# Seven products of quarters in both layers, tile 0's second layer in two parts around them, and some weights kept

## The chip, the cores and the metric

The kernel runs on one core of a Trainium2 chip. The metric is the device time of one execution in microseconds (us). TensorE (PE) multiplies into PSUM; LDWEIGHTS (PEld) loads its stationary operand beside it. VectorE (DVE), ScalarE (ACT) and GpSimd (POOL) do elementwise work, and SyncE (SP) issues nearly all DMA transfers from one queue. All engines run their own instruction list in order and wait for each other through semaphores.

## What is computed

Inputs are fp32: q, k, v of 2 batches x 8 heads x 768 positions x 64, and for two layers a w_in of 512x2048 and a w_out of 2048x512. The outline of the reference:

```
scores_l = scale * q @ k.T, kept where |i-j| < 16        # window
scores_s = scale * q @ max_of_32(k).T + log(32)          # block summaries
x = softmax([scores_l, scores_s]) @ [v, mean_of_32(v)]   # x: 1536 x 512
h = x @ moe_w_in;  x = max(h, 0)**2 @ moe_w_out          # layer 0
h = x @ moe2_w_in; out = (h * sigmoid(1.702 * h)) @ moe2_w_out   # layer 1
```

## The kernel before

The 1536 tokens are three tiles of 512 (t = 0, 1, 2), the 2048 hidden columns 16 blocks of 128 (f). Every fp32 operand is split into a high and a low fp32r part (xh and xl, gh and gl, two weight tiles w each), and every product of blocks is three matmuls, hi*hi, hi*lo and lo*hi, of 128x128 on 128x512. One `step(m, t, f)` (L733) is layer m, tile t, block f: 12 matmuls of x with w_in (L743) into one PSUM bank, the activation, the split into gh and gl (L767 to L773), and in `finish()` (L778, one step later) 12 matmuls with w_out (L791 in layer 0, L793 in layer 1), which add to four banks over all 16 blocks.

A weight block is loaded as raw 512 KB (`fetch`, L662), scaled in place by ACT (L678), shifted and merged by DVE (L682, L685), and split by `parts` (L704: a cast on ACT or DVE, L709 or L710, and a subtraction on DVE or POOL, L714). There are 28 weight tiles (`NW`, L630), 16 of them beside the attention and 12 in memory that comes free when it ends; raw blocks have three buffers.

For layer 1, tiles 0 and 1, `pairs` (L866) takes two tiles and two blocks at a time as a 2x2 product of quarters and makes it with seven products instead of eight (L895), each 6 matmuls. Sums of quarters come first (`operands` L819 for the tokens, `prep_pair` L833 for the weights, helper `add` L692). Partial sums pass through bank `a` four times; after each of the first three, `keep` (L911, a copy, mostly on ACT, L307) takes the bank's value before the next product adds to it, and `sum_to` (L903) adds on DVE. The pair's first tile is finished in the loop, the second one in `late` (L946), which holds 12 matmuls per block.

The main sequence (L973 to L990): the attention together with layer 0 of tile 0, in the order of the table `ORDER` (L27; `k`, `q`, `v` are loads, `sv` the block means of v by matmul, L436, `tk` and `tq` transposes, L457, `h` and `t` the two ends of a 128-row attention block, `w` weight blocks, `s` and `S` steps). Then layer 0 of tile 1 and tile 2 in plain steps, `pairs` for layer 1 of tiles 0 and 1, `late` for tile 1, and plain steps for layer 1 of tile 2. A planner (`Plan`, L113) gives each operation a start on its engine from costs written into the kernel, lets `soonest` choose between two engines (`LEAN` adds to DVE's end), and the instructions are emitted in the order of these starts. TensorE also gets small matmuls on a constant (L996) in planned gaps before the first dense work.

Of the kernel before, what the change touches and what calls it, by code (L numbers as in the profile page):

```python
# [10 lines left out]
F32 = mybir.dt.float32  # L11
F32R = mybir.dt.float32r
U32 = mybir.dt.uint32
AF = mybir.ActivationFunctionType
# [13 lines left out]
    k,0,1 k,1,1 sel k,2,1 tk,0 tk,1 q,1,1 q,0,1 tk,2 pk,0 m,1 sv,0 m,0 tq,1 m,2 pk,1 tq,0 v,0 q,3,1 v,1  # L28
    h,0,0 q,2,0 w,3,0 h,0,1 h,3,0 h,1,0 h,1,1 ps,0 t,0 w,0,0 v,2 h,2,0 w,0,1 w,2,0 v,3 h,2,1 h,3,1 t,1 w,2,1
    tq,2 pk,2 s,0,0 w,3,1 v,4 t,2 w,1,0 t,3 s,3,0 h,4,0 k,3,1 s,2,0 s,2,1 w,1,1 tk,3 h,5,0 s,0,1 sv,1 s,3,1  # L30
    s,1,0 w,6,0 v,5 k,5,1 tq,3 k,4,0 w,6,1 w,4,0 tk,4 h,4,1 tk,5 s,1,1 pk,5 S,6 t,4 v,6 w,4,1 h,5,1 w,5,0
    w,5,1 w,10,0 q,4,0 S,4 S,5 w,7,0 v,7 w,10,1 w,7,1 pk,3 S,10 pk,4 t,5 tq,4 S,7 ps,1 w,14,0 w,8,0 h,7,0
    w,8,1 w,9,0 w,11,0 v,8 h,6,0 h,7,1 S,8 h,6,1 h,9,0 w,14,1 S,14 q,5,0 t,7 h,9,1 w,11,1 w,9,1 tq,5 S,11
    t,6 w,12,0 v,9 h,11,0 h,11,1 h,10,0 S,9 t,9 v,10 v,11 w,15,0 w,12,1 h,8,0 S,12 t,11 w,13,0 w,13,1 h,10,1
    h,8,1 w,15,1 S,15 t,10 S,13 t,8
# [77 lines left out]
class Plan:  # L113
# [11 lines left out]
    LEAN = {"DVE": 0.5}  # L125
# [67 lines left out]
    def soonest(self, choices, reads=(), writes=(), after=()):  # L193
# [60 lines left out]
def kernel(  # L254
# [375 lines left out]
    NA, NW = 4 * RING, 4 * RING + 12  # L630
# [6 lines left out]
    def end_attention():  # L637
# [91 lines left out]
    ended = set()  # L729
    first_ops = {}  # L730
    pending = []

    def step(m, t, f, c0, c1, first, last):  # L733
# [14 lines left out]
        wt.release(wih, wil)  # L748
        wt.held |= {woh.name, wol.name}
# [280 lines left out]
```

## Time and profile before

| | |
|---|---|
| median of 3 runs | 599.99 us (599.25 to 603.17) |
| the profiled execution's own time | 599.57 us |
| its span, first to last instruction | 597.8 us |
| mean granted TensorE clock, share of full speed | 0.996 |
| PE busy | 582.0 us, 97% of the span, 3472 matmuls |
| DVE, ACT, POOL busy | 498.8, 418.7, 66.3 us |
| moved by DMA | 104.58 MB, mean 175 GB/s |

The profile is of one execution. Busy times count overlapping instructions of an engine once, and ends of matmuls are modelled, so that waits are read from the list of waits, and the pace of matmuls from the starts in the timeline. "Idle before" names what ended the wait.

### The profile page before, as it was taken

How to read it: one execution, taken by the hardware profiler on the slowest of the kernel's cores; microseconds unless marked ns; L12 is line 12 of the kernel's file. 1: busy time of each engine (PE TensorE's matmuls, PEld its weight loads, DVE VectorE, ACT ScalarE, POOL GpSimd, SP SyncE). 2: the span in 40 equal slices, each digit the busy share in tenths (PEclk: the TensorE clock that was granted, in tenths of full speed). 3: DMA queues.
4: the chain of work that ended last, by engine and by line, in shares of the span. 5: the costliest groups of instructions: out<-in, count | busy, mean ns of one | idle time of the engine just before them, and what ended most of it. 6: DMA issues, size and time to landing. Idle time of an engine off the chain costs nothing.

```text
span 597.8 us, 9872 instructions
## 1 busy us (share of the span) xinstructions
PE 582.0 (97%) x3472; PEld 484.5 (81%) x3472; DVE 498.8 (83%) x1065; ACT 418.7 (70%) x848; POOL 66.3 (11%) x129
## 2 busy tenths in 40 slices
PE   7799999999999999999999999999999999999997
PEld 6588988788888888888888888888888888888885
DVE  4788898879889777698676799999999999899992
ACT  6888797788877777764787776667776545665543
POOL 5121100023110000020001212211110000000000
PEclk9989999999999999999999999999999999999999
DMA  9999988834537655522565513434445766766641
GB/s 242 230 249 261 255 210 234 203 113 132 151 101 242 210 172 186 209 70 70 178 212 194 158 47 108 157 123 133 142 148 182 241 192 214 252 187 200 185 133 70
DMA packets 95313, 104.58 MB, mean 175 GB/s; under 512 B 29792, under 2 KB 82016, under 8 KB 95264
## 3 DMA queue, kind: packets, MB, share of 16 engines
q1 hardware_dynamic: 94944, 103.17, 58.2%
q0 software_dynamic: 320, 0.79, 0.6%
q8 instruction: 27, 0.44, 0.3%
q14 instruction: 22, 0.18, 0.1%
HBM read 100.01 MB, written 3.15 MB: 173 GB/s over the span
## 4 chain that ended last, share of the span: by engine, by line
PE 86%; DMA 7%; ACT 3%; DVE 2%; issue 1%; SPq 0%; POOL 0%; DVEq 0%; ACTq 0%
PE acc L791 12%; PE acc L793 11%; PE acc L743 11%; PE m L793 9%; PE h L743 8%; PE m L743 7%; PE acc L895 7%; PE m L791 5%; PE h L895 4%; DMA raw<-in_moe_w_in_dram 2%; PE m L895 2%; PE h L793 2%; PE h L791 2%; PE m L598 2%; DMA qin<-in_q_dram 1%; DMA kin<-in_v_dram 1%
## 5 line engine op out<-in xcount | busy, mean ns | idle before, releaser
L678 ACT ACTIVATE raw<-raw 128x512 f32<-128x512 f32 x164 | 108.1, 678 | 21.8 <-DMA raw<-in_moe_w_in_dram 11.3
L685 DVE SCALAR_TENSOR_TENSOR xw<-raw,xw 128x512 uint32<-128x512 uint32 x164 | 112.7, 693 | 6.0 <-ACT raw L678 2.0
L714 DVE TENSOR_TENSOR w<-xw,w 128x512 fp32r<-128x512 f32 (+1 forms) x167 | 114.9, 695 | 2.6 <-ACT w L709 0.8
L709 ACT CAST w<-xw 128x512 fp32r<-128x512 f32 (+1 forms) x129 | 77.3, 608 | 36.7 <-DVE xw L685 36.3
L791 PE MATMUL acc<-gh,w 128*128 128x512 f32 (+1 forms) x288 | 81.7, 368 | 1.0 <-DVE xl L611 1.0
L682 DVE TENSOR_SCALAR xw<-raw 128x512 uint32<-128x512 uint32 x164 | 69.6, 426 | 15.1 <-DMA raw<-in_moe_w_out_dram 11.5
L743 PE MATMUL h<-xh,w 128*128 128x512 f32 (+1 forms) x224 | 69.6, 370 | 1.0 <-DVE xl L611 1.0
L771 DVE TENSOR_TENSOR gl<-r,gh 128x512 fp32r<-128x512 f32 (+1 forms) x68 | 45.9, 674 | 25.8 <-ACT gh L769 25.6
L743 PE MATMUL acc<-xh,w 128*128 128x512 f32 x192 | 63.0, 389 | 0.0
L791 PEld LDWEIGHTS acc<-gh,w 128*128 128x128 f32 x288 | 51.9, 188 | 10.1 <-DVE xl L611 1.2
L793 PE MATMUL acc<-w,gh 128*128 128x512 f32 x192 | 59.2, 389 | 0.0
L791 PE MATMUL acc<-gl,w 128*128 128x512 f32 (+1 forms) x144 | 52.7, 366 | 0.0
L793 PE MATMUL m<-w,gh 128*128 128x512 f32 x160 | 49.3, 389 | 0.0
L743 PEld LDWEIGHTS h<-xh,w 128*128 128x128 f32 x224 | 40.7, 188 | 8.5 <-ACT pT L307 1.2
L769 ACT CAST gh<-r 128x512 fp32r<-128x512 f32 (+1 forms) x66 | 39.7, 602 | 6.4 <-DVE r L765 4.8
L793 PEld LDWEIGHTS acc<-w,gh 128*128 128x128 f32 x192 | 36.1, 188 | 7.6
L743 PEld LDWEIGHTS acc<-xh,w 128*128 128x128 f32 x192 | 36.1, 188 | 7.5
L743 PE MATMUL m<-xh,w 128*128 128x512 f32 x128 | 42.0, 389 | 0.0
L743 PE MATMUL h<-xl,w 128*128 128x512 f32 (+1 forms) x112 | 40.3, 360 | 0.0
L793 PE MATMUL acc<-w,gl 128*128 128x512 f32 x96 | 37.3, 389 | 0.0
L743 PE MATMUL acc<-xl,w 128*128 128x512 f32 x96 | 37.3, 389 | 0.0
L558 ACT ACTIVATE sm<-sm,st 128x120 f32<-128x120 f32 x96 | 36.6, 385 | 0.8 <-DVE st L549 0.8
(181 smaller groups left out, 1111.4 us busy)
## 6 DMA issues: line engine op xcount, KB each, us to landing
raw<-in_moe_w_out_dram SPq DMA_DIRECT2D x90, 512.0 KB, 3.7
raw<-in_moe_w_in_dram SPq DMA_DIRECT2D x74, 512.0 KB, 3.9
vw<-in_v_dram SPq DMA_DIRECT2D x20, 192.0 KB, 6.1
kin<-in_v_dram SPq DMA_DIRECT2D x6, 512.0 KB, 7.3
out_dram<-r SPq DMA_DIRECT2D x12, 256.0 KB, 2.1
kin<-in_k_dram SPq DMA_DIRECT2D x5, 512.0 KB, 5.6
qin<-in_q_dram SPq DMA_DIRECT2D x3, 512.0 KB, 7.3
qin<-in_q_dram SPq DMA_DIRECT2D x6, 256.0 KB, 6.7
```

Of the source, the lines that this page charges most:

```text
L558: nc.scalar.activation(out=s.t[:, h, :], in_=s.t[:, h, :], func=AF.Exp, bias=st.t[:, 0, h:h + 1], scale=-1.0, accum_out=st.t[:, 1, h:h + 1])
L678: nc.scalar.activation(out=top, in_=top, func=AF.Prelu, scale=-(2.0 ** -80), alpha=-(2.0 ** -32))
L682: op("DVE", 0.36, lambda: nc.vector.tensor_scalar(out=x.t, in0=raw.t[:, :, 0], scalar1=29, scalar2=None, op0=ALU.logical_shift_right), rea ...
L685: op("DVE", 0.64, lambda: nc.vector.scalar_tensor_tensor(out=x.t, in0=raw.t[:, :, 1], scalar=3, in1=x.t, op0=ALU.logical_shift_left, op1=A ...
L709: plan.soonest([("ACT", 0.09 + 0.44 * fr, False, lambda: nc.scalar.copy(out=hi.t[:, hc], in_=src())), ("DVE", 0.05 + 0.4 * fr, True, lambd ...
L714: eng.tensor_tensor(out=lo.t[:, lc], in0=src(), in1=hi.t[:, hc].bitcast(F32), op=ALU.subtract)
L743: nc.tensor.matmul(hp.t[:, cols], lhsT=w.t[:, kc * P:(kc + 1) * P], rhs=x.t[:, kc, cols], start=(kc == 0 and n == 0), stop=(kc == KC - 1 a ...
L769: ("ACT", da - 0.1, False, lambda: nc.scalar.copy(out=gh.t[:, cols], in_=r.t[:, cols]))],
L771: op("DVE", dd, lambda: nc.vector.tensor_tensor(out=gl.t[:, cols], in0=r.t[:, cols], in1=gh.t[:, cols].bitcast(F32), op=ALU.subtract), rea ...
L791: nc.tensor.matmul(a.t[:, cols], lhsT=w.t[:, j * P:(j + 1) * P], rhs=g.t[:, cols], **st)
L793: nc.tensor.matmul(a.t, lhsT=g.t[:, j * P:(j + 1) * P], rhs=w.t, **st)
L895: nc.tensor.matmul(bank.t, lhsT=a, rhs=rhs(b, kh), start=(begin and k == 0 and n == 0), stop=(k == 1 and n == 2), skip_group_check=True)
```

## The change

Layer 0 of tiles 1 and 2 now goes through `pairs` and `late` too, and layer 1 takes the pair (2, 1). Tile 0's second layer runs in plain steps, in two parts: 10 blocks before layer 0's pairs, 6 behind layer 0's `late`. The first part's output is copied into four tiles `part` and added on DVE at the end (`parted`). While such a part runs, `operands_first` makes the sums of quarters for the pairs that follow and prepares their first weights, one piece per step (`beside`). The first two blocks of each `pairs` use split weights that are still there (`keep_w`, `kept_w`), with sums made from the parts (`add(x0, h0, l0)`); the last pair's w_out stay for `late`, which goes through the blocks backwards; tile 2's fp32 output of layer 0 is copied from PSUM for its sums (`kept`). `pairs` has no step pending when it begins, and prepares the next pair's weights as soon as a pair's own are released. The activation of layer 1 is one ACT instruction (`Gelu_apprx_sigmoid`) instead of a sigmoid on ACT and a multiplication on DVE. The subtraction for gl may go to POOL. Weight tiles are 24 instead of 28. The planner's lean on DVE is split, and becomes 1.5 against ACT and 0.25 against POOL behind the attention. `ORDER` is a new table; what it moves is shown by the order of the instructions. The diff, cut to its core:

```diff
...
+            if eng == "DVE":
+                end += self.lean[0] if choices[0][0] == "ACT" else self.lean[1]
...
-    NA, NW = 4 * RING, 4 * RING + 12
+    NA, NW = 4 * RING, 4 * RING + 8
...
-    def layer(m, t, order, halfway=None):
+        for i, b in enumerate(part_of):
+    def layer(m, t, order, beside=iter(())):
...
-            step(m, t, f, 0, TT, [n == 0] * 2, [n == NF - 1] * 2)
-            if halfway and n == 3:
-                halfway()
+            step(m, t, f, 0, TT, [n == 0] * 2, [n == len(order) - 1] * 2)
+            if n >= 2:
+                next(beside, None)
+        for _ in beside:
+            pass
...
+        if (m, f) in keep_w:
+            kept_w[m, f] = w_sb[m, f]
+            stay.update(id(b) for b in w_sb[m, f])
+            wt.held |= {b.name for b in w_sb[m, f]}
+        else:
...
-            op("ACT", da, lambda: nc.scalar.activation(out=r.t[:, cols], in_=hp.t[:, cols], func=AF.Sigmoid, scale=1.702),
+            op("ACT", da, lambda: nc.scalar.activation(out=r.t[:, cols], in_=hp.t[:, cols], func=AF.Gelu_apprx_sigmoid),
                reads=[(hp, 0)], writes=[(r, 0)])
-            op("DVE", dd, lambda: nc.vector.tensor_tensor(out=r.t[:, cols], in0=hp.t[:, cols], in1=r.t[:, cols],
-                                                          op=ALU.mult), reads=[(hp, 0)], writes=[(r, 0)])
...
-        op("DVE", dd, lambda: nc.vector.tensor_tensor(out=gl.t[:, cols], in0=r.t[:, cols],
-                                                      in1=gh.t[:, cols].bitcast(F32), op=ALU.subtract),
-           reads=[(r, 0), (gh, 0)], writes=[(gl, 0)], port=True)
+        plan.soonest([(e, d, True, lambda eng=eng: eng.tensor_tensor(
+            out=gl.t[:, cols], in0=r.t[:, cols], in1=gh.t[:, cols].bitcast(F32), op=ALU.subtract))
+            for e, d, eng in (("DVE", dd, nc.vector), ("POOL", 0.06 + 1.2 * fr, nc.gpsimd))],
+            reads=[(r, 0), (gh, 0)], writes=[(gl, 0)])
...
+                   reads=[(xh[t], key) for key in keys] + [(a, 0)], writes=[(xl[t], key) for key in keys])
+                if t == 2:
+                    b = gs[8 * (j % 2) + 2 * (j // 2)]
+                    op("ACT", 0.48, lambda a=a, b=b: nc.scalar.copy(out=b.t, in_=a.t), reads=[(a, 0)], writes=[(b, 0)])
+                    kept.add((t, j))
+            elif (t, 0) in parted:
+                copy(lambda j=j: part_of[j].t, lambda a=a: a.t, a, [(part_of[j], 0)])
+                del acc[m, t, j]
...
+                if (t, 1) in parted:
+                    op("DVE", 0.6, lambda j=j, ob=ob, a=a: nc.vector.tensor_tensor(
+                        out=ob.t, in0=a.t, in1=part_of[j].t, op=ALU.add),
+                       reads=[(a, 0), (part_of[j], 0)], writes=[(ob, 0)])
...
-            for b, t, kc in ((x12, tb, k), (x11, ta, k), (x22, tb, 2 + k), (x21, ta, 2 + k)):
-                plan.soonest([(e, d, True, lambda eng=eng, b=b, t=t, kc=kc: eng.tensor_tensor(
...
-            for i, (o, x, y) in enumerate(((t1, x12, x11), (t2, x22, t1), (t3, x22, x12), (t4, x21, t2))):
+
+            def less(i, o, x, y):
                 add(o, ALL, x, ALL, y, ALL, sub=True)
                 parts(o, ALL, tops[4 * i + k], ALL, tops[4 * i + 2 + k], ALL)
 
...
+            whole(x12, tb, k)
+            whole(x22, tb, 2 + k)
+            yield
+            less(2, t3, x22, x12)
+            yield
+            whole(x11, ta, k)
...
+    def prep_pair(m, f0, f1):
...
+        if (m, f0) in kept_w:
+            (h0, l0), (h1, l1) = (kept_w[m, f][:2] for f in (f0, f1))
+            w = [wt.hold() for _ in range(4)]
+            x0, x1, s12, s34 = (xw_ring.take() for _ in range(4))
+            add(x0, ALL, h0, ALL, l0, ALL)
+            add(x1, ALL, h1, ALL, l1, ALL)
+            w22 = h1, l1, H, H
...
+    def prep_all(m, f0, f1):
+        w = prep_pair(m, f0, f1)
+        w2 = []
+        for f in (f0, f1):
+            if (m, f) in kept_w:
+                hi, lo = kept_w.pop((m, f))[2:]
+            else:
+                hi, lo = wt.hold(), wt.hold()
...
+    def operands_first(m, ta, tb, f0, f1):
+
+        for i, _ in enumerate(operands(ta, tb)):
+            if i == 8:
+                ready.append(prep_all(m, f0, f1))
+            yield
...
-        g = tmp.take() if sb else out
-        op("ACT", 0.64, lambda: nc.scalar.activation(out=g.t, in_=src.t, func=AF.Sigmoid, scale=1.702),
-           reads=[(src, key)] if sb else rd, writes=[(g, 0)])
-        op("DVE", 0.6, lambda: nc.vector.tensor_tensor(out=out.t, in0=src.t, in1=g.t, op=ALU.mult),
-           reads=rd + ([(g, 0)] if sb else []), writes=[(out, key)], port=sb)
...
+        op("ACT", 0.64, lambda: nc.scalar.activation(out=out.t, in_=src.t, func=AF.Gelu_apprx_sigmoid),
+           reads=rd, writes=[(out, key)])
...
-        for f in range(0, NF, 2):
-            w = prep_pair(m, f)
...
+        while pending:
+            finish()
+        fs = [(fs[i], fs[i + 1]) for i in range(0, NF, 2)]
+        ahead = ready.pop()
+        for f0, f1 in fs:
+            (w, left), w2 = ahead
...
-            sum_to(gs[f + 1], 0, c, u3)
+            sum_to(gs[f1], 0, c, u3)
             if pending:
                 finish()
...
+            product(a, left[5], 3, False)
+            product(c, left[6], 6, False)
+            sum_to(gs[f0], 0, c, u2)
...
+            first, last = (f0, f1) == fs[0], (f0, f1) == fs[-1]
+            if last:
+                ahead = None
+                for f, (hi, lo) in zip((f0, f1), w2):
+                    kept_w[m, f] = [None, None, hi, lo]
+                    stay.update((id(hi), id(lo)))
+            else:
+                ahead = prep_all(m, *fs[fs.index((f0, f1)) + 1])
...
+    def late(m, t, fs):
+
+        for f in reversed(fs):
+            if (m, f) in kept_w:
+                hi, lo = kept_w.pop((m, f))[2:]
+            else:
...
+    plan.lean = 1.5, 0.25
     banks.release(banks.last["h0"])
-    layer(0, 1, [f for f in range(NF) if not any(b.dead for b in w_sb[0, f])]
-          + [f for f in range(NF) if any(b.dead for b in w_sb[0, f])])
-    layer(0, 2, reversed(range(NF)), lambda: operands(0, 1))
-    pairs(1, 0, 1)
-    late(1, 1)
-    layer(1, 2, range(NF))
-    finish()
+    while pending:
+        finish()
+    parted.add((0, 0))
+    one = [f for f in range(NF) if (0, f) in kept_w]
+    one += [f for f in range(NF) if f not in one]
+    two = list(range(NF))
+    layer(1, 0, two[:1:-1][:10], operands_first(0, 1, 2, *one[:2]))
+    pairs(0, 1, 2, one)
+    late(0, 2, one)
+    keep_w.update({(1, two[0]), (1, two[1])})
+    layer(1, 0, two[:1:-1][10:] + two[1::-1], operands_first(1, 2, 1, *two[:2]))
+    pairs(1, 2, 1, two)
+    late(1, 1, two)
+    while pending:
+        finish()
```

SP's queue near its start, where the loads of the attention stand (vw are windows of v, kin from in_v what the block means are made of, qin and kin from in_k the units of q and k, 128x8x128 is 512 KB). Before:

```order
L379 DMA qin_190<-in_q_dram 128x8x128
L428 DMA kin_209<-in_v_dram 128x8x128
L428 DMA kin_232<-in_v_dram 128x8x128
L428 DMA kin_255<-in_v_dram 128x8x128
L410 DMA vw<-in_v_dram 80x8x64
L410 DMA vw<-in_v_dram 96x8x64
L379 DMA qin_347<-in_q_dram 128x8x128
L410 DMA vw<-in_v_dram 96x8x64 x2
L385 DMA qin_422<-in_q_dram 128x8x64 x2
L669 DMA raw_461<-in_moe_w_in_dram 128x4x256
```

and of the change:

```order
L380 DMA qin_173<-in_q_dram 128x8x128
L411 DMA vw<-in_v_dram 80x8x64
L411 DMA vw<-in_v_dram 96x8x64
L386 DMA qin_240<-in_q_dram 128x8x64 x2
L380 DMA qin_300<-in_q_dram 128x8x128
L675 DMA raw_340<-in_moe_w_in_dram 128x4x256
L411 DMA vw<-in_v_dram 96x8x64 x2
L429 DMA kin_382<-in_v_dram 128x8x128
L429 DMA kin_422<-in_v_dram 128x8x128
L429 DMA kin_439<-in_v_dram 128x8x128
L386 DMA kin_469<-in_k_dram 128x8x64 x2
```

The three loads for the block means of v moved from ahead of the first windows, the third unit of q and the first weights to behind them.

ACT, where the load of an activation table stands that layer 1 needs (raw is a weight block, r an activation or a kept value, acc and h PSUM banks). Before it is in the first pair:

```order
L709 CAST w_4108<-xw_4085 128x512 [waits Pool_49]
L678 ACTIVATE raw_4065<-raw_4065 128x512 [waits DMAHW2_49]
L307 COPY r_4122<-acc_4081 128x512 [waits PE_49]
L861 ACT_TABLE_LOAD
L861 ACTIVATE r_4129<-r_4110 128x512 [waits DVE_49]
L307 COPY r_4149<-acc_4081 128x512 [waits PE_49]
L307 CAST xh_2109<-acc_3317 128x512 [waits PE_49]
```

and of the change it is in the first step of tile 0's second layer, behind the wait for that step's bank h:

```order
L715 CAST w_2432<-xw_2316 128x512 [waits DVE_49]
L684 ACTIVATE raw_2311<-raw_2311 128x512 [waits DMAHW2_49]
L684 ACTIVATE raw_2352<-raw_2352 128x512 [waits DMAHW3_49]
L778 ACT_TABLE_LOAD [waits PE_49]
L778 ACTIVATE r_2452<-h_2423 128x512 [waits Activation_49]
L782 CAST gh_2460<-r_2452 128x512 [waits Activation_49]
L715 CAST w_2471<-xw_2376 128x512 [waits DVE_49]
```

The table load moved to an earlier stage, and there it stands between a PSUM bank's last matmul and the activation that reads it.

PE in the first pair, behind the product that bank acc_4081 (before) and acc_2989 (change) gets third; the fourth adds to the same bank after `keep` has copied it. Before, the last three rows of the third and the first of twelve rows of a step's second product:

```order
L895 MATMUL acc_4081<-top_3461,w_3984 128x512
L895 MATMUL acc_4081<-top_3471,w_3984 128x512
L895 MATMUL acc_4081<-top_3461,w_3992 128x512
L791 MATMUL acc_3317<-gh_4069,w_3883 128x512
L791 MATMUL acc_3317<-gh_4069,w_3893 128x512
L791 MATMUL acc_3317<-gl_4078,w_3883 128x512
```

and of the change:

```order
L981 MATMUL acc_2989<-top_2848,w_2976 128x512
L981 MATMUL acc_2989<-top_2857,w_2976 128x512
L981 MATMUL acc_2989<-top_2848,w_2985 128x512
L981 MATMUL acc_3069<-xh_1203,w_3022 128x512
L981 MATMUL acc_3069<-xl_1239,w_3022 128x512
L981 MATMUL acc_3069<-xh_1203,w_3038 128x512
L981 MATMUL acc_2989<-top_2737,w_2078 128x512
L981 MATMUL acc_2989<-top_2746,w_2078 128x512
L981 MATMUL acc_2989<-top_2737,w_2088 128x512
```

Three matmuls of the next pair's first product (acc_3069) now stand where twelve of a pending step stood.

## Rows read from the trace of the kernel before

**Rows 1.** Stretches: length, busy us per engine (count), granted clock, DMA share, GB/s.
```profile
0.00:75.00 75.00, 64.24 (x777) 57.89 (x778) 56.51 (x191) 59.07 (x167) 18.85 (x71) 0.98 1.05 248
168.00:345.00 177.00, 177.00 (x783) 146.61 (x782) 138.21 (x244) 130.89 (x219) 14.90 (x14) 1.00 0.50 164
345.00:465.00 120.00, 119.97 (x529) 98.87 (x528) 111.87 (x194) 82.46 (x145) 18.87 (x19) 1.00 0.42 135
465.00:508.00 43.00, 43.00 (x191) 35.61 (x191) 41.50 (x78) 21.28 (x35) 0.00 (x0) 1.00 0.66 209
508.00:585.00 77.00, 77.00 (x342) 63.77 (x341) 69.61 (x127) 43.50 (x73) 0.00 (x0) 1.00 0.60 186
```
**Rows 2.** PE's waits, whole span: who for whom, us in total, times, longest.
```profile
PE acc L457 <- DMA qin<-in_q_dram: 3.1, 3, 1.7
PE acc L586 <- DVE sm L565: 1.5, 3, 0.7
```
**Rows 3.** The chain that ended last, in order of time: start, us, what.
```profile
168.95 2.72 PE acc L791 x12
400.54 4.08 PE acc L895 x18
```
**Rows 4.** DMA issues: operation, count, KB each, median us to landing.
```profile
raw<-in_moe_w_in_dram SPq DMA_DIRECT2D x74, 512.0 KB, 3.9
vw<-in_v_dram SPq DMA_DIRECT2D x20, 192.0 KB, 6.1
```
**Rows 5.** Timeline, PE, in the attention: start, us, what, count [idle before].
```profile
39.17 0.35 PE L743 MATMUL h<-xh,w 128*128 128x256 f32 x1 [1.05 <-DVE xl L611]
69.08 0.60 PE L457 MATMUL m<-ident,kin 128*128 128x128 f32 x4
121.39 1.03 PE L586 MATMUL m<-ident,sm 128*120 128x128 f32 x8
165.44 1.25 PE L598 MATMUL m<-pT,vw 120*64 120x64 f32 x32
```
**Rows 6.** Timeline, ACT, at the table load of the first pair.
```profile
345.03 1.28 ACT L861 ACT_TABLE_LOAD   x1
346.33 0.63 ACT L861 ACTIVATE r<-r 128x512 f32<-128x512 f32 x1
```
**Rows 7.** Timeline of one step's activation in layer 1, tile 2.
```profile
577.03 0.39 PE L743 MATMUL acc<-xh,w 128*128 128x512 f32 x1
577.45 0.60 ACT L763 ACTIVATE r<-acc 128x512 f32<-128x512 f32 x1 [1.69 <-PE acc L743]
578.09 0.69 DVE L765 TENSOR_TENSOR r<-acc,r 128x512 f32<-128x512 f32 x1 [0.36 <-ACT r L763]
578.81 0.62 ACT L769 CAST gh<-r 128x512 fp32r<-128x512 f32 x1 [0.20 <-DVE r L765]
579.75 0.68 DVE L771 TENSOR_TENSOR gl<-r,gh 128x512 fp32r<-128x512 f32 x1
```
**Rows 8.** Timeline in the first pairs: a cast, a keep, and the product behind it.
```profile
356.88 0.62 ACT L709 CAST w<-xw 128x512 fp32r<-128x512 f32 x1 [1.43 <-DVE xw L685]
357.40 0.58 ACT L307 COPY r<-h 128x512 f32<-128x512 f32 x1
358.04 1.65 PE L895 MATMUL h<-top,w 128*128 128x512 f32 x6
359.78 0.59 ACT L307 COPY r<-h 128x512 f32<-128x512 f32 x1 [0.69 <-PE h L895]
```
**Rows 9.** Timeline, DVE, one block of late.
```profile
471.36 0.42 DVE L682 TENSOR_SCALAR xw<-raw 128x512 uint32<-128x512 uint32 x1
471.86 0.69 DVE L714 TENSOR_TENSOR gl<-gs,gh 128x512 fp32r<-128x512 f32 x1
472.47 0.68 DVE L714 TENSOR_TENSOR w<-xw,w 128x512 fp32r<-128x512 f32 x1
473.07 0.68 DVE L685 SCALAR_TENSOR_TENSOR xw<-raw,xw 128x512 uint32<-128x512 uint32 x1
```

More of the change, by code (lines that the diff above doesn't have):

```diff
@@ L124 @@
     LAND = 0.95
-    LEAN = {"DVE": 0.5}
+    lean = 0.5, 0.5
     def __init__(self):
@@ L650, in end_attention @@
             b.after, b.make = [attn_end], lambda i=i: pool_b().tile([P, TT], F32R, tag=f"top{i}", name=f"top{i}")
-    def layer(m, t, order, halfway=None):
+        for i, b in enumerate(part_of):
+            b.after, b.make = [attn_end], lambda i=i: pool_b().tile([P, TT], F32, tag=f"part{i}", name=f"part{i}")
+    def layer(m, t, order, beside=iter(())):
         while len(pending) > 1:
             finish()
+        order = list(order)
         for n, f in enumerate(order):
@@ L729 @@
     ended = set()
+    keep_w, kept_w, stay = set(), {}, set()
+    parted = set()
+    kept = set()
+    part_of = [fixed(None, "", None) for _ in range(4)]
     first_ops = {}
@@ L798, in finish @@
                 first_ops.setdefault(ACC[j], []).append(o)
-        wt.release(woh, wol)
+        wt.release(*(b for b in (woh, wol) if id(b) not in stay))
         ended.update((m, t, h) for h in halves if last[h])
@@ L814, in finish @@
                 r0 = t * TT + j * P
[L815 removed]
+                if (t, 1) in parted:
[3 more added lines that the diff above has]
+                else:
+                    copy(lambda ob=ob: ob.t, lambda a=a: a.t, a, [(ob, 0)])
                 plan.dma(0.8, lambda r0=r0, ob=ob: nc.sync.dma_start(out=out[r0:r0 + P, :], in_=ob.t),
                    reads=[(ob, 0)])
+        if m == 1 and (t, 0) in parted:
+            parted.remove((t, 0))
+            parted.add((t, 1))
+            ended.difference_update([(m, t, 0), (m, t, 1)])
     def operands(ta, tb):
@@ L877, in rhs, with product @@
             return b.t if b in tops else b.t[:, kc, :]
-        for f in range(0, NF, 2):
-            w = prep_pair(m, f)
-            w2 = []
-            for x in range(2):
-                hi, lo = wt.hold(), wt.hold()
-                parts(fetch(m, f + x, 1), ALL, hi, ALL, lo, ALL)
-                w2.append((hi, lo))
-            def product(bank, hi, lo, c, i, begin):
+        while pending:
[4 more added lines that the diff above has]
+            (w, left), w2 = ahead
+            def product(bank, operand, i, begin):
+                hi, lo, *c = operand
                 for k in range(2):
@@ L940, in pairs @@
                 parts(r, ALL, gh, ALL, gl, ALL)
-                pending.append((m, ta, 0, TT, [f + x == 0] * 2, [f + x == NF - 1] * 2, *w2[x], gh, gl))
+                pending.append((m, ta, 0, TT, [first and x == 0] * 2, [last and x == 1] * 2, *w2[x], gh, gl))
             banks.release(a, b, c)
-            for x in range(2):
-                act(m, gs[f + x], True, 0, gs[f + x])
-    def late(m, t):
-        for f in range(NF):
-            hi, lo = wt.hold(), wt.hold()
-            parts(fetch(m, f, 1), ALL, hi, ALL, lo, ALL)
+            for f in (f0, f1):
+                act(m, gs[f], True, 0, gs[f])
+    def late(m, t, fs):
+        for f in reversed(fs):
+            if (m, f) in kept_w:
+                hi, lo = kept_w.pop((m, f))[2:]
+            else:
+                hi, lo = wt.hold(), wt.hold()
+                parts(fetch(m, f, 1), ALL, hi, ALL, lo, ALL)
             while len(pending) > 1:
@@ L954, in late @@
             parts(gs[f], ALL, gh, ALL, gl, ALL)
-            pending.append((m, t, 0, TT, [f == 0] * 2, [f == NF - 1] * 2, hi, lo, gh, gl))
+            pending.append((m, t, 0, TT, [f == fs[-1]] * 2, [f == fs[0]] * 2, hi, lo, gh, gl))
+            stay.difference_update((id(hi), id(lo)))
     steps = [0, 0]
@@ L971 @@
     )
+    blocks = {}
+    for item in ORDER.split():
+        if item[:2] == "w,":
+            blocks[int(item.split(",")[1]) % RING] = int(item.split(",")[1])
+    used = [int(item.split(",")[1]) for item in ORDER.split() if item[:2] in ("s,", "S,")]
+    keep_w.update((0, f) for f in sorted(blocks.values(), key=lambda f: used[::-1].index(f))[:2])
     attn_ops = []
```

81 lines of the change are left out of this document (49 added, 32 removed).

## The prediction

> **What bounds the kernel now.** I read the stretches first. From 168 to 585 us PE is busy all the time at the full clock, and DVE comes close to it only while `late` runs, 41.50 of 43.00 us [rows 1]. The list of PE's waits for the whole span holds a dozen entries, the longest sum 3.1 us, and all of them lie in the first 116 us; asked for the stretch from 116 us to the end, the list is empty [rows 2]. So behind the attention the kernel costs what its matmuls cost. The chain gives the pace: 12 matmuls in 2.72 us, 18 in 4.08, thus 0.2267 us for each of 512 columns, in a step as in a product of quarters [rows 3].
>
> Ahead of that the limit is another one. In the first 75 us the DMA share is 1.05 at 248 GB/s [rows 1]. There I compare the time at which PE reaches a place with the work that it has done by then, counted from the order, at prices from starts in the timeline: 0.2267 us for 512 columns, 0.117 for 256, about 0.11 for a transpose, 0.06 to 0.07 for a small matmul of the attention; the matmuls that only fill gaps count as nothing. The transposes of a later unit of k begin at 69.08 us behind 42.4 us of work, so 26.7 us are lost by then; the last attention block's product with v begins at 165.44 behind 133.8, 31.6 lost [rows 5]. Of the loss 27 us come in the time in which DMA is full, and 5 later.
>
> **PE's matmuls.** A pair of two tiles and two blocks takes 7 x 6 = 42 matmuls with w_in instead of 48. Layer 1 has its 8 pairs before and after; layer 0's 8 pairs are new: 8 x 6 = 48 matmuls less. 48 x 0.2267 = **10.9 us less**, all of it on PE and in the stretch where PE never waits [rows 1 to 3]. Nothing else of PE's dense work changes in number; tile 0's second layer in two parts has the same matmuls, and the sum of its parts is on DVE.
>
> **DVE and ACT.** They must stay under PE. The 48 multiplications of layer 1 go (0.69 us each [rows 7]), and of 164 weight blocks 148 are loaded and split. These cost nothing and give nothing as long as PE is the limit. Where DVE is fullest now is the first part of tile 0's second layer: 10 steps of 24 matmuls, 54.4 us of PE. Up to the last DVE result that this part waits for, the order has 57 operations on two 512-column operands, 17 merges and 16 shifts. By starts in `late` one of them takes 0.61, 0.72 and about 0.4 us [rows 9], so 34.8 + 12.2 + 6.4 = 53.4 us: under PE, by a margin as in `late` before, where PE did not wait [rows 1, 2]. The second part has 39, 6 and 8 of them and some smaller ones, 33.5 us against 35.4 of PE. Layer 0's pairs have about 104 us of DVE and 96 of ACT against 119.7 of PE. I take **nothing** for all these; the price if that cover is gone is rival B. The new sums come early: weights in a new tile are asked for at least 16 us of PE work after the tile's last reader (26 before, with 28 tiles), and a load lands 3.9 us after its issue [rows 4].
>
> **The activation and its table.** Behind a step's last w_in matmul came sigmoid, multiplication, cast and subtraction: the matmul starts at 577.03, ACT at 577.45, gl is there at 580.43 [rows 7]. Without the multiplication it is 0.42 + 0.60 + 0.62 + 0.69 and some 0.14 between, 2.5 us, and PE has 0.23 + 2.72 + 0.45 = 3.4 us of other matmuls until it needs gl. How long the new function takes no row shows; the nearest are the sigmoid's 0.60 and 0.63 [rows 6, 7], I take those, and up to 1.5 us it would cost nothing. The Trainium skill (ScalarE: Activation LUTs, Step-by-step: what each stage is for) says that ACT's pace is the same whatever the function, which would give 0.60 too; no row before shows it for this function.
>
> The order has two table loads, as before, but the second one stands in the first of tile 0's steps behind the wait for its bank. It takes 1.28 us, and the activation follows at once [rows 6]. 2.5 + 1.28 - 3.4 = **0.4 us more**, once. The Trainium skill (ScalarE: Activation LUTs, What ACT_TABLE_LOAD costs) adds a drain of about 1.38 us to every switch; by that the sum would be 1.4 us higher. The row speaks against a drain behind the load, since the activation starts 0.02 us after it.
>
> **The first pairs.** `keep` copies bank a between products. In the row of the first pair the product of six starts at 358.04, its copy at 359.78 takes 0.59, and the one before let PE go on 0.06 us behind its end [rows 8]: some 1.1 us from the start of a last matmul to the next one on that bank. With six matmuls between (1.36 us) that is hidden; with three of the next pair (0.68) it leaves 0.2 us. The order has five such places and one with a longer chain (0.3 us), against about 0.2 us of the kind before: **1.1 us more**. Since nothing is pending when `pairs` begins, a gap there has no other cover.
>
> **The beginning.** The order's loads: to the unit of k at 69.08 us it was 24 of 512 KB, 4 of 256, 10 of 192 and 2 of 160, 15.9 MB. In the change the place with most bytes against the work ahead of it is the last of the second batch's block means of v: 17.0 MB, 49.1 us of work. 1.05 MB more at 248 GB/s are 4.2 us; 6.7 us more work is ahead: 2.5 us less lost. A weight block a little later gives the same (1.77 MB or 7.1 us more against 9.8 us of work). The first block means come 2.33 MB later, 9.4 us, but those were ready long before they were used: PE's first dense work began at 39.17 behind 15.7 us of work, 23.5 lost, and later places lose more anyway [rows 5]. What comes later (31.6 lost, against 26.7) I leave as it is. Bounds: 4.6 less if the later loss shrinks as well, 3.5 more if the table packs its second half worse. I take **2 us less**.
>
> **The sum.** 599.57 (the profiled execution, 0.4 us under the median) - 10.9 - 2 + 0.4 + 1.1 = 588.2; for the median 588.5 us.
>
> **Rivals.** A, the beginning gives the gain back: the loss falls at the loads but rises behind them, by 3.5 us over before. For it: ACT's copies of p stand alone between the last transposes and the last products, and the 31.6 us show that something there costs. Against it: the same work, and DMA is what binds first. 588.5 + 2 + 3.5 = 594.
>
> B, DVE falls behind in tile 0's two parts: if each operation took its whole length, 0.69 instead of 0.61 [rows 9], the first part would be 57.8 and the second 36.9 us, 3.4 and 1.5 over PE: 593.4. Against it: in a full queue the starts are 0.61 apart.
>
> C, the other side, ACT is late for the keeps. In the pairs a cast that stands ahead of a copy delays it: 357.40 instead of about 356.9, and the product waited until 358.04 [rows 8]. One cast ahead costs under 0.2 us, since 0.5 us of the 1.36 are spare; from two casts ahead on each late keep costs 0.65. Layer 0's pairs put relu and square on ACT, 96 us of 119.7, where ACT had 82.46 of 120 [rows 1]. 24 of the 48 keeps late by two casts are 15.6 us: 604, not faster, and slower if more of them are. Against it: the casts wait for DVE in between, so ACT seldom has two ready.
>
> D, the new activation is slow: over 1.5 us each step waits; at 2 us the 16 steps lose 8 us and layer 1's pairs are full on ACT, some 600.
>
> **Chances.** Forecast 0.72 (585 to 592 by its own bounds: the beginning from 4.6 less to nothing, the keeps from nothing to twice), A 0.12, B 0.06, C 0.07, D 0.03. One per cent, 6 us, is about what a measurement of this kernel can tell from no change. Under 594 lie the forecast, half of A and most of B: faster 0.85. Within 1% the rest of A and B and part of C and D: 0.10. Slower 0.05, from C and D. The range takes in half of A and all of B: 584.5 to 594.
>
> **What would show it.** Right: no PE wait over 0.5 us behind the attention, a pace of 2.72 us for 12, one wait for ACT behind the table load, PE waiting for copies in the first pair of each layer only. The last attention product is as far behind its counted work as 30 us. Wrong: PE waiting for DVE in the steps of tile 0 (B), for copies in every pair (C), a long gap or a lower clock ahead of the first dense matmul (A), or an activation over 1 us (D).

## The result, and the profile after

The changed kernel takes 593.36 us (median of 4 executions, 590.72 to 593.77), the kernel before 599.92 in the same comparison: a ratio of 0.9878, 95% interval 0.9856 to 0.9899. By the medians it is 6.6 us faster, where 11.5 were forecast. The profiled execution took 593.77 us, the highest of the four, with a span of 591.8.

The stretches of after, with the columns of [rows 1]; the last three are the first part of tile 0's second layer, layer 0's pairs and layer 1's pairs:

```profile
0.00:75.00 75.00, 59.79 (x706) 52.12 (x706) 52.22 (x182) 57.70 (x168) 25.31 (x81) 0.93 0.91 215
172.00:227.00 55.00, 55.00 (x241) 44.92 (x241) 51.35 (x92) 41.13 (x71) 0.00 (x0) 1.00 0.51 163
227.00:347.00 120.00, 120.00 (x525) 97.85 (x524) 101.97 (x195) 99.16 (x178) 8.50 (x7) 1.00 0.46 149
...
425.00:545.00 120.00, 120.00 (x529) 98.83 (x528) 104.01 (x194) 92.44 (x163) 9.01 (x8) 1.00 0.56 180
```

Behind the attention all is as forecast: PE busy throughout, DVE 51.35 of 55 us and ACT 99.16 of 120 where they are fullest. The first 75 us are not: the clock is 0.93 on the mean (0.98 before), and DMA, which was to bind, has a share of 0.91 (1.05 before). The list of PE's waits names who was late (waiter, whom for, us, times, longest); its first line, all others being of 2.3 us or less in total:

```profile
PE acc L599 <- DMA vw<-vs: 6.3, 2, 5.7
```

From 116 us on the list is empty, as before [rows 2]. This wait did not exist before. `vw<-vs` is the transfer from SBUF to SBUF that puts the block means of v beside the windows of v; the first product with v needs it. The chain of waits shows how it came about (start, us, what):

```profile
18.64 2.96 SPq L429
21.65 7.49 DMA kin<-in_v_dram
29.18 0.68 PE acc L437 x16
...
31.33 0.81 POOL vw L421
32.14 9.75 DMA vw<-vs
...
41.94 1.76 PE acc L599 x28
```

The loads for the means stand behind the windows in SP's queue, the last one lands at 29.14, the means are copied by 31.0, and POOL issues the transfers at 31.33 and 32.14. In the kernel before POOL issued them here (POOL's timeline, and the median time from issue to landing, first of before and then of after):

```profile
20.67 0.81 POOL L420 DMA_DIRECT2D vw<-vs  x1 [1.67 <-DVE st L572]
21.85 0.64 POOL L420 DMA_DIRECT2D vw<-vs  x1
...
vw<-vs POOLq DMA_DIRECT2D x4, 192.0 KB, 6.2
```

```profile
vw<-vs POOLq DMA_DIRECT2D x4, 192.0 KB, 9.2
```

Those medians are of four transfers. The two that the first products need took 5.3 and 7.1 us before, 9.6 and 9.8 now. The first product with v on PE, before and after, the latter with the last work ahead of it:

```profile
33.23 1.15 PE L598 MATMUL m<-pT,vw 120*64 120x64 f32 x32
```

```profile
34.55 0.65 PE L587 MATMUL m<-ident,sm 128*120 128x128 f32 x4 [1.65 <-DVE sm L566]
40.94 0.48 PE L599 MATMUL acc<-pT,vw 120*64 120x64 f32 x4 [5.74 <-DMA vw<-vs]
```

Before, the second transfer landed at 21.85 + 7.1, about 28.9, and the product began 4.3 us behind it. Now it is issued 10.3 us later and takes 2.7 longer: it lands at 41.9.

The wait costs a second time. PE's stretch from 36 to 46 us of after, clock behind the counts of the engines:

```profile
36.00:46.00 10.00, 4.54 (x67) 4.24 (x68) 2.41 (x5) 3.36 (x7) 2.10 (x5) 0.53 0.97 236
```

PE did 0.65 us of work between 32.9 and 35.2 and none from there on. The granted clock went to the lower level, 1.2 GHz, at about 36.7 us, and came back at 46.9: the 4.5 us of work between the first product and the first dense matmul took 7.5, of which 0.5 was a second wait and some 2.5 the clock. That agrees with the Trainium skill (TensorE: Matmul & The Clock Gate, HAM oscillation — how this bites in real kernels), by which work behind a wait for DMA is paid at the lower clock. The kernel before pays such a price too, behind a wait for a unit of q; it is part of the 23.5 us that it had lost at its first dense matmul. Its stretch from 29 to 33 us:

```profile
29.00:33.00 4.00, 3.16 (x15) 3.16 (x15) 2.04 (x4) 1.21 (x3) 0.99 (x1) 0.59 1.21 278
```

The time at which PE reaches a place, less the work counted up to there, as in the prediction, shows where the loss arises. These are the first dense matmul and two later products with v, the last one among them:

```profile
48.44 0.36 PE L753 MATMUL h<-xh,w 128*128 128x256 f32 x1
77.46 1.15 PE L599 MATMUL m<-pT,vw 120*64 120x64 f32 x32
169.45 1.19 PE L599 MATMUL m<-pT,vw 120*64 120x64 f32 x32
```

Behind 19.3, 45.5 and 134.5 us of work they are 29.1, 32.0 and 35.0 late; before it was 23.5 at the first dense matmul and 31.6 at the last product [rows 5]. So between these two profiles the beginning lost 3.4 us, where a gain of 2 was forecast.

Two small gaps remain behind it. At the table load, ACT and PE:

```profile
175.05 1.28 ACT L778 ACT_TABLE_LOAD   x1 [0.54 <-PE h L753]
176.34 0.60 ACT L778 ACTIVATE r<-h 128x512 f32<-128x512 f32 x1
```

```profile
177.30 0.39 PE L753 MATMUL acc<-xh,w 128*128 128x512 f32 x1
177.65 0.73 PE L807 MATMUL m<-w,gh 128*128 128x512 f32 x2
178.37 0.50 PE L807 MATMUL m<-w,gl 128*128 128x512 f32 x1
178.71 0.63 PE L807 MATMUL m<-w,gh 128*128 128x512 f32 x2
```

Four matmuls from 177.30 to 178.71 take 1.41 instead of 0.91, so 0.50 us. The new function takes 0.60, as the sigmoid did [rows 6, 7], and starts 0.01 us behind the load: no drain behind it, as forecast. And in the first pairs, PE with the copy on ACT that it waited for:

```profile
244.82 0.39 PE L805 MATMUL h<-gl,w 128*128 128x512 f32 x1
245.21 1.67 PE L981 MATMUL acc<-top,w 128*128 128x512 f32 x6
246.72 0.63 PE L805 MATMUL acc<-gh,w 128*128 128x512 f32 x2
```

```profile
244.57 0.59 ACT L308 COPY r<-acc 128x512 f32<-128x512 f32 x1 [0.60 <-PE acc L981]
```

The product starts 0.05 us behind the copy, 0.16 late, and takes 0.15 longer. There are five such places up to 273 us, spread over layer 0's first four pairs, and two from 431 to 437; taken together, start against start, they are 1.2 us in layer 0's pairs and 0.4 in layer 1's.

### The profile page after: what moved, and what is told of

Its sections match the earlier page's. It is cut to its first block, busy times and chain, and to the rows that moved or that the text cites. A ratio compares the mean times of both kernels' runs of the same rounds, so it can differ in the third digit from the quotient of the medians.

```text
span 591.8 us, 9749 instructions
## 1 busy us (share of the span) xinstructions
PE 572.3 (97%) x3418; PEld 474.3 (80%) x3418; DVE 477.4 (81%) x1033; ACT 441.0 (75%) x908; POOL 65.4 (11%) x125
## 4 chain that ended last, share of the span: by engine, by line
PE 88%; DMA 4%; DVE 3%; SPq 2%; ACT 1%; issue 1%; POOL 0%; DVEq 0%; POOLq 0%; ACTq 0%
PE acc L805 14%; PE acc L981 13%; PE acc L807 11%; PE m L981 10%; PE m L807 9%; PE h L753 8%; PE m L805 6%; PE acc L753 4%; PE h L981 4%; PE h L807 3%; PE m L753 2%; PE h L805 2%; DMA vw<-vs 2%; PE m L599 1%; DMA kin<-in_v_dram 1%; DMA qin<-in_q_dram 1%
## 5 line engine op out<-in xcount | busy, mean ns | idle before, releaser
L715 ACT CAST w<-xw 128x512 fp32r<-128x512 f32 (+1 forms) x164 | 96.9, 601 | 23.1 <-DVE xw L691 16.5
L684 ACT ACTIVATE raw<-raw 128x512 f32<-128x512 f32 x148 | 96.5, 674 | 9.6 <-DMA raw<-in_moe_w_in_dram 7.1
L753 PE MATMUL h<-xh,w 128*128 128x512 f32 (+1 forms) x184 | 55.1, 363 | 0.6 <-DVE r L769 0.5
L981 PE MATMUL acc<-top,w 128*128 128x512 f32 x186 | 47.4, 393 | 0.0
L715 ACT CAST gh<-gs 128x512 fp32r<-128x512 f32 x32 | 19.9, 622 | 35.5 <-PE h L807 25.4
L720 DVE TENSOR_TENSOR gl<-gs,gh 128x512 fp32r<-128x512 f32 x32 | 22.1, 691 | 28.5 <-ACT gh L715 27.9
L981 PEld LDWEIGHTS acc<-top,w 128*128 128x128 f32 x186 | 34.5, 188 | 8.9 <-ACT r L308 1.7
L720 POOL TENSOR_TENSOR w<-xw,w 128x512 fp32r<-128x512 f32 x13 | 17.5, 1346 | 194.4 <-ACT w L715 182.5
L981 PE MATMUL m<-top,w 128*128 128x512 f32 x138 | 35.3, 391 | 0.0
L807 PEld LDWEIGHTS m<-w,gh 128*128 128x128 f32 x156 | 29.2, 188 | 6.3 <-ACT gh L782 0.4
```

What stands on the lines that cost most here:

```text
L684: nc.scalar.activation(out=top, in_=top, func=AF.Prelu, scale=-(2.0 ** -80), alpha=-(2.0 ** -32))
L715: plan.soonest([("ACT", 0.09 + 0.44 * fr, False, lambda: nc.scalar.copy(out=hi.t[:, hc], in_=src())), ("DVE", 0.05 + 0.4 * fr, True, lambd ...
L720: eng.tensor_tensor(out=lo.t[:, lc], in0=src(), in1=hi.t[:, hc].bitcast(F32), op=ALU.subtract)
L753: nc.tensor.matmul(hp.t[:, cols], lhsT=w.t[:, kc * P:(kc + 1) * P], rhs=x.t[:, kc, cols], start=(kc == 0 and n == 0), stop=(kc == KC - 1 a ...
L807: nc.tensor.matmul(a.t, lhsT=g.t[:, j * P:(j + 1) * P], rhs=w.t, **st)
L981: nc.tensor.matmul(bank.t, lhsT=a, rhs=rhs(b, kh), start=(begin and k == 0 and n == 0), stop=(k == 1 and n == 2), skip_group_check=True)
```

## The experiments

Each loss named below is that at the last product with v, counted as above, from the kernel's own profile.

**The table.** The new kernel with the old table, and the old kernel with the new table:

```diff
-    sel k,1,1 m,0 k,0,1 m,1 k,2,1 tk,0 q,0,1 ...
+    k,0,1 k,1,1 sel k,2,1 tk,0 tk,1 q,1,1 ...
```

> The changed kernel with the attention's table of before, all else as changed. Theory 1 (the new table is what cost: the first product with v waits for the block means, whose loads it put behind others): the loss at the last product with v falls from 35.0 back to about 31.6 us, so 593.4 - 3.4 = 590.0, no wait over 2 us for vw<-vs, first dense matmul near 39 us. Rival 2 (the loss comes from the new work behind the attention and the table is neutral): 593.4. Behind the attention both expect the 2.0 us of gaps that the changed kernel shows.

Measured 592.95 us, ratio 0.9874 (0.9845 to 0.9903): 0.4 us under the change by the medians, which is no difference.

> The kernel before with the new table alone. Theory 1: the same wait of about 6 us for vw<-vs, first dense matmul near 48 us, 599.9 + 3.4 = 603.3. Rival 2 (table neutral): 599.9. Rival 3 (the new table helps and the rest of the change cost more than its matmuls saved): under 598.

Measured 601.87 us, ratio 1.0027 (1.001 to 1.0044). The second comparison settles the sign: the new table alone makes the old kernel 1.4 us slower by the medians, 0.6 to 2.6 by the interval, and it brings the same wait with it:

```profile
40.16 0.48 PE L598 MATMUL acc<-pT,vw 120*64 120x64 f32 x4 [5.07 <-DMA vw<-vs]
```

Its loss is 35.1, like that of after. The 1.4 us are less than the 3.4 between the two profiles: this profile and that of after are of the slowest execution of their kernel. In the first comparison theory 1 missed. Its profile has no wait for `vw<-vs` and 29.0 us lost up to 99 us, less than after, and yet 35.0 at the end. PE's timeline and clock around 117 us show where the rest went:

```profile
116.62 1.04 PE L536 MATMUL m<-kw,qT 64*64 64x120 f32 x30 [1.55 <-DVE st L550]
```

```profile
115.00:120.00 5.00, 3.45 (x37) 2.77 (x37) 4.79 (x24) 4.97 (x22) 0.48 (x2) 0.78 0.46 129
120.00:125.00 5.00, 5.00 (x22) 4.02 (x22) 4.79 (x25) 3.96 (x15) 0.45 (x2) 0.88 0.35 101
```

Here a weight block landed late (ACT scales it at 111.58; at 109.79 in the kernel before, where PE was 0.8 us further on), the exponentials queued behind it on ACT, DVE was late with the masks, PE waited 1.55 us, and the clock was at the lower level for some 3.4 of the ten us shown. In the profile before the same wait was 0.5 us long and the clock stayed at 1.00. So the old table has a weak place of its own, and its loss is not a constant: 31.6 in one profile, 35.0 in this. Whether the new table costs anything in the changed kernel, these two kernels alone don't show.

**gl on POOL.** With the old table, and DVE alone for gl in the steps, the attention's instructions stand in the order of before on every engine:

```diff
-        plan.soonest([(e, d, True, lambda eng=eng: eng.tensor_tensor(
...
+        op("DVE", dd, lambda: nc.vector.tensor_tensor(out=gl.t[:, cols], in0=r.t[:, cols],
```

> The old table and, for gl in the steps, DVE alone as before: the attention is then instruction for instruction that of before, and only what follows it is changed. Theory A (the choice of POOL for gl shifted the attention, and what follows it gains 48 matmuls less 2.0 us of gaps): before minus 8.9, ratio 0.985, loss at the last product with v 31.6 in an undisturbed execution. Rival B (POOL for gl is neutral; the old table's own stall at 115 us, which cost 4.5 us in the last run and 1.9 in the profile of before, comes and goes by itself): same as with POOL, 593.0.

Measured 591.39 us, ratio 0.9857 (0.984 to 0.9875). That is the gain of the part behind the attention with the beginning's order held: 8.7 us, against 10.9 for the 48 matmuls less the gaps of 1.8. The profiles say the same: from the last product with v to the end it is 432.4 us in the kernel before and 423.6 here, 8.8 less. PE waited neither at 115 us, where the clock stayed at 1.00, nor for `vw<-vs`; the loss was 32.6.

In the changed kernel, POOL taken out of the choice only for the steps beside the attention:

```diff
-            for e, d, eng in (("DVE", dd, nc.vector), ("POOL", 0.06 + 1.2 * fr, nc.gpsimd))],
+            for e, d, eng in (("DVE", dd, nc.vector), ("POOL", 0.06 + 1.2 * fr, nc.gpsimd))[:1 if m + t == 0 else 2]],
```

> The changed kernel with DVE alone for gl in the steps beside the attention, POOL still allowed behind it. With the old table this part made 1.6 us. Theory A (a gl on POOL takes 1.3 us instead of 0.7 and stands between copies there, whatever the table): 591.8. Rival B (only the old table's stall at 115 us was sensitive to it): 593.4.

Measured 591.99 us, ratio 0.9874 (0.9846 to 0.9902). Both medians are 1.4 to 1.6 us under the kernels with POOL, but the intervals overlap; whether POOL costs anything there stays open. With DVE alone the new table is 0.6 us over the old one, which the intervals don't separate either.

**The wait itself.** Block means of the first batch copied by ACT and DVE from PSUM to their place, across partitions, without the transfer:

```diff
...
+            if b == 0:
+                banks.release(vs[b])
+                for p in range(NPAIR):
+                    copy(lambda p=p, r0=r0, c=c: vw_all[r0:r0 + NSUM, :, c, p * P:(p + 1) * P],
+                         lambda p=p: vs[b].t[32 * p:32 * p + NSUM, 0:P].unsqueeze(1).to_broadcast([NSUM, NV, P]),
+                         vs[b], [(vs_rows[n], (c, p)) for n in range(NV)])
+                continue
...
```

> The changed kernel, with the first batch's block means copied from PSUM straight into the operand of the products with v by ACT and DVE (8 copies) in place of 4 small copies and a DMA from SBUF to SBUF that took 9.7 us. Theory 1 (that DMA, late and behind full queues, holds the first product): no wait for vw<-vs, first product with v near 36 us instead of 40.9, clock not below 1.0 for more than 3 us, and some 3 us less at the end: 590.4. Rival 4 (the DMA queues are the limit anyway, so the next place waits as long): first product earlier but the loss at 77 us is 32 again: 593.4.

Measured 590.08 us, ratio 0.983 (0.9805 to 0.9854), under the interval of the changed kernel. The first product with v begins at 31.35, waits 2.1 us in all for the copies, and the first dense matmul and the last product come at

```profile
40.58 0.36 PE L764 MATMUL h<-xh,w 128*128 128x256 f32 x1 [0.45 <-DVE st L584]
164.80 1.19 PE L610 MATMUL m<-pT,vw 120*64 120x64 f32 x32
```

The loss is 30.3, 4.7 less than in the profile of after. The clock was at the lower level here too, for some 3.4 us between 35 and 39 us, so that part of the price stayed. The plan was made anew around the copies, so this is the transfer with all that hung on it. The best kernel measured here is this one.

The clock's share of the wait, by 26 more matmuls on the constant ahead of the first product (the timeline has two records for each):

```diff
+        if i == 1:
+            for n in range(26):
+                w = Op()
+                w.eng, w.fn, w.seq, w.far, w.start = "PE", lambda: keep_warm(), 0, False, pv_op.start - 1e-6
+                w.end = w.start
+                plan.ops.append(w)
```

> The changed kernel with 26 more matmuls on the constant (5.7 us at full clock) ahead of the first product with v, in the wait. Theory 1a (of the loss, 3.0 us are the halved clock from 36.7 to 46.5 us: 4.5 us of work took 7.5): clock 1.0 throughout, first dense matmul near 45.5 instead of 48.4, 590.4. Theory 1b (the wait for the data alone counts, and what follows waits for DMA anyway): 593.4.

Measured 592.09 us, ratio 0.9865 (0.9841 to 0.9889). The clock stayed up, though the product came no earlier than in after:

```profile
34.00:48.40 14.40, 13.17 (x202) 1.00 0.97 218
```

```profile
35.72 5.97 PE L1114 MATMUL warm<-ident 128*128 128x128 f32 x52
41.62 1.15 PE L599 MATMUL acc<-pT,vw 120*64 120x64 f32 x32
```

The loss is 32.6, 2.4 less than after; by the medians it is 1.3 us, which the intervals don't separate. So by the profiles the clock's share of the loss is some 2.4 us; the medians don't show it. The copies' 4.7 us can't be divided that way, since their run kept a stretch at the lower clock.

**The activation and the lean.** Sigmoid and multiplication again:

```diff
-            op("ACT", da, lambda: nc.scalar.activation(out=r.t[:, cols], in_=hp.t[:, cols], func=AF.Gelu_apprx_sigmoid),
+            op("ACT", da, lambda: nc.scalar.activation(out=r.t[:, cols], in_=hp.t[:, cols], func=AF.Sigmoid, scale=1.702),
                reads=[(hp, 0)], writes=[(r, 0)])
+            op("DVE", dd, lambda: nc.vector.tensor_tensor(out=r.t[:, cols], in0=hp.t[:, cols], in1=r.t[:, cols],
+                                                          op=ALU.mult), reads=[(hp, 0)], writes=[(r, 0)])
...
```

> The changed kernel with the activation of layer 1 in two instructions again (sigmoid on ACT, multiplication on DVE: 16 in the steps, 32 in the pairs). Theory A (DVE's margin in tile 0's two parts is as small as counted): 10 x 0.61 us more make the first part 59.5 against 54.4 of PE, the second 37.2 against 35.4, together 6.9 us: 600.3, with PE waiting for gl or for the sums there. Rival B (the planner moves other work to ACT and POOL, which have room): 593.4 and no wait over 0.5 us.

Measured 607.29 us, ratio 1.0131 (1.0107 to 1.0155): 13.9 slower than the change and slower than before. The waits of PE from 116 us on, and the three stretches that lost (first part, layer 0's pairs, layer 1's pairs):

```profile
PE acc L753 <- DVE w L720: 2.6, 4, 0.9
PE m L986 <- ACT r L308: 2.5, 3, 1.7
PE acc L809 <- ACT gh L715: 1.7, 1, 1.7
```

```profile
172.00:232.00 60.00, 56.78 (x240) 43.97 (x239) 56.26 (x100) 33.53 (x56) 0.00 (x0) 1.00 0.47 147
232.00:352.00 120.00, 117.93 (x511) 94.97 (x511) 104.61 (x199) 98.83 (x177) 9.56 (x9) 1.00 0.44 145
430.00:550.00 120.00, 115.53 (x501) 92.98 (x500) 113.68 (x205) 84.78 (x147) 11.81 (x13) 1.00 0.43 141
```

The first part loses 5.1 us more than in after, as counted: ten multiplications of 0.61 put DVE over PE. The second part, where 1.8 us had been counted, lost nothing. The pairs lose some 9 more, 6 of them at the start of layer 1's, where PE waits for copies and a cast on ACT while DVE is busy 113.68 of 120 us. That was not counted.

> The changed kernel with the planner's lean as before (0.5 against both ACT and POOL behind the attention). Theory A (DVE is under PE everywhere by the count, lean or not): 593.4. Rival B (the lean of 1.5 is what keeps DVE under PE in tile 0's parts, 53.4 of 54.4 us): PE waits for DVE there, 1 to 5 us, 595 to 598.

With `plan.lean = 1.5, 0.25` left out it measured 595.12 us, ratio 0.9925 (0.9899 to 0.9952). No wait for DVE, but one for ACT's copies in the first pairs of layer 0:

```profile
PE acc L981 <- ACT r L308: 1.4, 3, 0.7
```

Neither theory holds: DVE keeps up, and ACT is late with the `keep` copies. The trace has 3 us of gaps there instead of 1.2; by the medians the kernel is 1.8 us over the change, and the two intervals meet at 0.9899.

**The small gaps, and a surprise.** A one-column activation with the new function behind the last exp brings the table in early, and layer 0's pairs begin with a step pending; on top of the means by copy:

```diff
...
-        while pending:
+        while pending and m:
...
+    tiny = Buf([], lambda: work.tile([P, 1], F32, tag="tiny", name="tiny"))
+    op("DVE", 0.1, lambda: nc.vector.memset(tiny.t, 0.0), writes=[(tiny, 0)])
+    op("ACT", 1.4, lambda: nc.scalar.activation(out=tiny.t, in_=tiny.t, func=AF.Gelu_apprx_sigmoid),
+       writes=[(tiny, 0)], after=[max(last_exp, key=lambda o: o.end)])
```

> The block means by copy as in the run before, and two more edits: a one-column activation with the new function behind the last exp, so that the table load stands ahead of layer 1, and layer 0's pairs begin with a step of tile 0 still pending. Theory A: the gap of 0.50 us at the first step of layer 1 and the 1.5 us of gaps in layer 0's first pair are gone, 590.1 - 2.0 + 0.5 (layer 1's first pair still has its 0.5) = 588.6. Rival B (the load delays the attention's last copies by 1.3 us, or the pending step's banks come late): 590 or more.

Measured 599.68 us, ratio 0.9992 (0.9983 to 1.0002): 9.6 slower than the means by copy alone. Rival B's number holds, but of its reasons little is seen: the last product with v begins 1.7 us later, and the rest is lost behind it. PE's only wait behind 116 us is 0.4 long. The gap at the table load is gone, those of the first pairs have only moved to the second pair, and every matmul is slower. The chain, first with the small tile, then without it:

```profile
571.52 1.39 PE m L818 x6
572.91 0.70 PE acc L818 x3
```

```profile
570.12 1.36 PE acc L818 x6
571.48 0.68 PE m L818 x3
```

Three runs on the tile's size followed. The first has 16 columns (64 bytes a partition) instead of one, the second has 16 too, with gl on DVE in the attention and without the pending step, and the third is the second with 32 columns (128 bytes):

```diff
-    tiny = Buf([], lambda: work.tile([P, 1], F32, tag="tiny", name="tiny"))
+    tiny = Buf([], lambda: work.tile([P, 16], F32, tag="tiny", name="tiny"))
```

> The run before it (means by copy, table early, step pending; 599.7) again, with one number changed: the one-column tile that the early activation writes has 16 columns, so that it takes 64 bytes of a partition instead of the 32 that one column took, and the tiles behind it start at multiples of 64 bytes again. Theory A (the 9.6 us came from the tiles' place: behind it 12 matmuls of such tiles took 2.80 us instead of 2.72): the pace is 2.72 again and the time 589.6, that of the means by copy less 0.5 for the table load. Rival B (the early table load or the pending step cost it): 599.7 again.

> Means by copy, table load early with the 64-byte tile, gl on DVE in the attention, no step pending. If each part keeps what it gave alone: 590.1 - 0.5 - 1.6 = 588.0. If the parts give the same gain twice (the attention stays bound by its loads): 589.6.

> All parts together as in the run of 596.2, with 32 columns in the small tile: the tiles behind it start at multiples of 128 bytes again, as in every kernel that ran 12 matmuls in 2.72 us, and are moved by 128. Theory A (it is the 128 bytes): 2.72 again everywhere, 588.0 to 589.6. Rival B (any move of the tiles, or the early table load itself, costs it): 596.

They measured 596.68 (ratio 0.9948, 0.9931 to 0.9965), 596.21 (0.9937, 0.9912 to 0.9961) and 596.63 us (0.994, 0.9919 to 0.9962). With 64 bytes 3 us come back, with 128 nothing more, and the pace of the kernels without the tile in none: both theories A fall. Rival B of the first is missed too, that of the third came; of the two values expected for the second neither did, by 8.2 and 6.6 us. In the last one PE has no wait behind 116 us and the last product with v begins 0.5 us later than with the means by copy, but the chain still runs at

```profile
571.75 1.40 PE acc L818 x6
573.15 0.70 PE m L818 x3
```

## Why the prediction was right and wrong

The measured 593.36 lies in the stated range (584.5 to 594.0) and the sign is right, but it is outside the forecast's own 585 to 592. For the two profiled executions the terms as measured close: 599.57 - 10.9 + 3.4 + 1.8 = 593.9, against 593.77. By the medians the same sum, 599.92 - 10.9 + 1.8 = 590.8, leaves some 2.5 us to the beginning, 0.5 to 3.0 by the interval.

- **PE's matmuls, 10.9: right.** With the attention's order as before, the rest of the change gave 8.7 by the medians and 8.8 in the profiles, against 10.9 less the gaps, 9.1.
- **The gaps, 0.4 + 1.1: right in place, a little small.** 0.50 at the table load, 1.2 and 0.4 in the pairs, less 0.3 that the kernel before had: 1.8. In layer 0 the places are not in the first pair only, as the list of signs has it. The place with the pending step did not matter as I thought: with it, the gap moved.
- **DVE and ACT, nothing: right, by a margin that was real.** DVE is busy 51.35 of 55 us in the first part, and ten multiplications more cost there the counted 5 us. What I called giving nothing is a condition of the change: with the activation in two instructions the same kernel is slower than before. Rivals B, C and D did not happen.
- **The beginning, 2 us less: wrong, 3.4 more between the profiles, some 2.5 by the medians.** The step that failed is the sentence that the first block means come 9.4 us later "but those were ready long before they were used". I set them against the first dense matmul, at 39.17; their first user is the first product with v, at 33.23, and the second of the transfers that carry them was issued at 21.85 and took 7.1. The slack was 4.3 us, not "long". 9.4 - 4.3 gives some 5 us of wait from the trace of before; the wait was 5.7, and 0.5 for the second transfer. Bytes against work was the wrong measure for a load behind which a second transfer and a waiting product hang. Nor did I price the clock behind a wait: 2.4 us of the loss by the run with more matmuls in the wait, in the profiles alone. Of the 2.5 us by the medians, the new table made 1.4 in the old kernel, clear of noise; gl on POOL, which the sum had at nothing, may have made 1.4 more (3.4 became 2.0 in the profile without it), but the intervals don't separate that.
- **Rival A** gave 594 and came nearest, but not by its mechanism: it has the loss rise behind the loads, and here it rose at them, and fell from 5.6 to 3.4 over before behind them. What it named as a sign, a lower clock ahead of the first dense matmul, is there, but the kernel before has one too (0.59 from 29 to 33 us).

Open: how much of after's loss comes from gl on POOL and how much from the table, and why the old table's weak place at 115 us cost 4 us in one profile, 2 in another and 1 in the third (the landing of one block was late in the first; why it was is not shown).

## What to carry to other kernels

When an order of loads is changed, take each load to its first user, through every transfer and copy between, and set the new landing against the user's start in the trace; bytes against total work finds only the mean bound. A wait of TensorE can cost more than its length, as the one of 5.7 us did here: read the granted clock behind each wait. Filling the wait kept the clock up, though what it gave, 1.3 us by the medians, is not clear of noise; removing it gave 3.3, which is. Where a price is read from two profiles, set it beside the medians: 3.4 us between the profiles were 1.4 for the table alone. Work that is "hidden" should be tested by putting it back: here one multiplication per block was the difference between 593 and 607 us.

## What the runs showed of the hardware

- ACT and DVE copy 24 partitions of PSUM to another partition offset of SBUF, four tiles at once, in 0.58 us on ACT and 0.69 on DVE. Eight such copies beat two transfers of 192 KB that took 9.6 and 9.8 us behind full queues.
- Four kernels with a small tile and an early activation on it run PE slower everywhere: 512 columns take 0.230 to 0.233 us instead of 0.2267, with the granted clock at 1.00 and, behind 116 us, no wait over 0.4 us. From the last product with v to the end that is 6.8 us with 128 bytes and 8.5 with one column. The table load is not the cause, since the slower pace is there before it. With the one-column tile, three groups of three matmuls ahead of the load (their first rows), then the load and the activation:

```profile
154.37 0.63 PE L816 MATMUL acc<-gh,w 128*128 128x512 f32 x2
...
155.07 0.63 PE L816 MATMUL acc<-gh,w 128*128 128x512 f32 x2
...
155.77 0.63 PE L816 MATMUL acc<-gh,w 128*128 128x512 f32 x2
...
166.52 1.28 ACT L1099 ACT_TABLE_LOAD   x1
167.81 0.20 ACT L1099 ACTIVATE tiny<-tiny 128x1 f32<-128x1 f32 x1
```

  The groups are 0.70 apart; without the tile they are 0.68 to 0.69. The activation runs later still. What is left is the place of the other tiles, which the small one moves, or something else in the changed program; no run separates them, and the cause stays open.
